# A complex-gated linear attention with a GEGLU layer behind it: group 5's q and k turned by TensorE in place of transposing DMAs, one PSUM copy per turned group, and a new written order

## The chip, the cores and the metric

One core of one Trainium2 chip. A core has five engines that run side by side, each through its own instructions in order, and wait for one another by semaphores: TensorE (PE; its weight loads are shown apart as PEld), VectorE (DVE), ScalarE (ACT), GpSimd (POOL) and SyncE (SP). SP computes nothing; its queue issues DMAs, as POOL's does too. The metric is the device time of one execution in microseconds: the median of several runs, and beside it one execution under the hardware profiler.

## The reference

```python
# q, k, v, a_re, a_im: 4 batches x 8 heads x 768 steps x 48
mag = sqrt(a_re**2 + a_im**2)
scale = minimum(mag, 0.999) / (mag + 1e-06)
ar, ai = a_re * scale, a_im * scale
for t in range(S):                       # one 48 x 48 state per batch and head
    new_re = ar[t] * S_re - ai[t] * S_im
    new_im = ar[t] * S_im + ai[t] * S_re
    S_re, S_im = new_re + outer(k[t], v[t]), new_im
    y[t] = q[t] @ S_re
x = y as (4 * 768) x (8 * 48)
ffn = (gelu(x @ w_gate) * (x @ w_val)) @ w_out      # 384 -> 1536 -> 384
out = x + sigmoid(x @ w_res) * ffn
```

The gates are a complex number of modulus under one for each step, head and row of the state. The kernel doesn't step through time. It takes log and angle of the gates, sums them along time by matmuls with triangular matrices, and multiplies q by the running product and k by its inverse, with cosine and sine; within a block of steps attention is then a masked product of q and k, and a state is carried from block to block.

## The kernel before

The 768 steps of four batches are cut into 12 groups of 256 steps: group p is batch p mod 4, stretch p div 4. A group has two chunks c of 128 steps. Eight units of the second layer follow: units 0 to 3 take one group each (0 to 3), units 4 to 7 two each (4 and 5, 6 and 7, 8 and 9, 10 and 11).

All work is cut into named steps (`Steps.add`), and a string `ORDER` (L288) names the steps in the order in which they are written out, for all engines at once. No scheduler moves anything: each engine runs its steps in the order of that string (L946), and waits where the data or a buffer isn't ready. A dictionary `eo` in `PARAMS` says for many steps which engine does them. The names have the group or unit first, then the chunk, then the half of the heads.

- Loads, issued by SP: `Lar`, `Lai`, `Lq`, `Lk`, `Lvf`, 192 KB each. `VC` casts v to bf16. Weights, issued by POOL: `Wg0` to `Wg3`, `Wv0` to `Wv3`, `Wr`, `Wo0` to `Wo2`. `HOLDW` and `HOLDO` (L909) are one-element copies on POOL that wait for a certain load, so that what POOL issues behind them starts later.
- Gates (L539): squares `SQR`, `SQI`; their sum `ADD` on DVE; logarithms and exponentials `LNR`, `EXR`, `LM` and the arctangent `ATN` on ACT; the ratio `TH` on DVE; sums along time `CSL` (log) and `CST` (angle) on PE; from CSL `EX` and `EI` on ACT (the tiles E and Ei); from CST `OFF` (ACT or DVE) and `FR` and `ABS` on DVE, then `SIN` and `COS` on ACT. `CR`, `CD` carry the angle, and `DR`, `DS`, `DE`, `DI`, `DT`, `ML`, `ME`, `MM`, `MN` the moduli, from one stretch to the next.
- `log`, `trig` and `gelu` in the order load ACT's table for what follows (L949).
- Products (L700): `QE`, `KE` multiply q and k by E and Ei, `QR`, `KR` by cosine and sine into the tiles padQ and padK, all on DVE.
- Turning q and k: groups 0 to 4 on PE. `TP` makes eight 128x96 transposes for four heads, q's into the first half of a PSUM bank and k's into the second (L745), and two `CP` copies of 96x512, each on an engine of its own, bring them to the tile qk. From group `turn` = 5 on, `QT` and `KT` (L718) are transposing DMAs, one for a whole group's q and one for its k, into QT and KT.
- Attention (L722): `AT` multiplies turned q and k (L759), `AM` masks on DVE (L762), `DK` forms the new part of the state, `MI`, `ED`, `EN`, `EB` bring the state forward, `Y` forms the output of a chunk and `X` copies it to x. x is turned by PE for groups 0 to 4 (`XT`, copy `XC`) and by a transposing DMA from SP from group 5 on (`XD`, L829).
- The second layer (L824): `GP` and `VP` multiply by w_gate and w_val (L848), `GE` is the GELU on ACT, `HM` the product on DVE (L859), `RP` and `SG` the residual gate, `OP` the product with w_out (L873), `OT` and `RX` the last two elementwise steps, `ST` the store.

Tiles come from rings: a pool has as many buffers as `bufs` says, and each new tile takes the next one. PSUM has four banks in one ring (`psM`, tag mm) for CSL, CST, GP, VP, RP, OP, TP and XT, two for AT and one each for Y and DK.

Of the kernel before, what the change touches and what calls it, by code (L numbers as in the profile page):

```python
# [10 lines left out]
FP = mybir.dt.float32  # L11
# [7 lines left out]
 'turn': 5,  # L19
# [34 lines left out]
 'cpe': ('ACT', 'DVE'),  # L54
# [10 lines left out]
 'eo': {'CP0.0.0.0': 'ACT',  # L65
        'CP0.0.0.1': 'DVE',
        'CP0.0.1.0': 'ACT',
        'CP0.0.1.1': 'DVE',
        'CP0.1.0.0': 'DVE',
        'CP0.1.0.1': 'DVE',  # L70
        'CP0.1.1.0': 'ACT',
        'CP0.1.1.1': 'DVE',
        'CP1.0.0.0': 'DVE',
        'CP1.0.0.1': 'DVE',
        'CP1.0.1.0': 'DVE',
        'CP1.0.1.1': 'ACT',
# [24 lines left out]
        'CP4.1.0.0': 'DVE',
        'CP4.1.0.1': 'ACT',
        'CP4.1.1.0': 'DVE',
        'CP4.1.1.1': 'DVE',
        'CRA10': 'DVE',
        'CRA11': 'DVE',
        'CRA4': 'POOL',
        'CRA5': 'POOL',
        'CRA6': 'POOL',
        'CRA7': 'POOL',  # L110
        'CRA8': 'DVE',
        'CRA9': 'POOL',
# [4 lines left out]
        'CRB4': 'POOL',  # L117
        'CRB5': 'POOL',
        'CRB6': 'DVE',
        'CRB7': 'DVE',  # L120
        'EB10': 'POOL',
# [3 lines left out]
        'EB6': 'DVE',  # L125
        'EB7': 'POOL',
        'EB8': 'POOL',
        'EB9': 'ACT',
# [3 lines left out]
        'EN5': 'DVE',  # L132
# [3 lines left out]
        'EN9': 'POOL',  # L136
        'MM10': 'DVE',
        'MM11': 'DVE',
# [3 lines left out]
        'MM7': 'DVE',  # L142
        'MM8': 'POOL',
        'MM9': 'DVE',
        'MN10': 'POOL',
        'MN11': 'POOL',
        'MN4': 'POOL',
        'MN5': 'POOL',
        'MN6': 'POOL',
        'MN7': 'DVE',  # L150
        'MN8': 'POOL',
        'MN9': 'POOL',
        'OFF0.0': 'DVE',
# [60 lines left out]
        'SQR0.0': 'DVE',  # L214
        'SQR0.1': 'ACT',
        'SQR1': 'DVE',
        'SQR10': 'ACT',
        'SQR11': 'DVE',
        'SQR2': 'DVE',
        'SQR3': 'DVE',  # L220
        'SQR4': 'ACT',
        'SQR5': 'DVE',
        'SQR6': 'ACT',
        'SQR7': 'DVE',
# [4 lines left out]
        'VC1.0': 'DVE',  # L229
# [3 lines left out]
        'VC11.0': 'POOL',  # L233
        'VC11.1': 'ACT',
        'VC2.0': 'POOL',
        'VC2.1': 'POOL',
# [4 lines left out]
        'VC5.0': 'POOL',  # L241
        'VC5.1': 'ACT',
        'VC6.0': 'POOL',
        'VC6.1': 'POOL',
        'VC7.0': 'DVE',
        'VC7.1': 'POOL',
        'VC8.0': 'POOL',
        'VC8.1': 'ACT',
        'VC9.0': 'ACT',
        'VC9.1': 'POOL',  # L250
        'X0.0': 'ACT',
        'X0.1': 'ACT',
        'X1.0': 'ACT',
# [5 lines left out]
        'X2.0': 'ACT',  # L259
# [4 lines left out]
        'X4.1': 'ACT',  # L264
        'X5.0': 'DVE',
        'X5.1': 'ACT',
# [8 lines left out]
        'XC0.0': 'ACT',  # L275
        'XC0.1': 'ACT',
# [4 lines left out]
        'XC3.0': 'DVE',  # L281
        'XC3.1': 'DVE',
        'XC4.0': 'DVE',
# [82 lines left out]
class Steps:  # L366
# [24 lines left out]
def kernel(  # L391
# [15 lines left out]
    DD = 2 * D  # L407
# [574 lines left out]
```

## Time and profile before

| | |
|---|---|
| median of 3 runs | 274.76 us (274.43 to 276.25) |
| profiled execution | 275.13 us, span 273.4 us |
| PE busy | 234.9 us (86%) |
| DVE busy | 222.7 us (81%) |
| ACT busy | 207.9 us (76%), of it 34 table loads 43.6 us |
| POOL busy | 114.7 us (42%) |
| mean granted TensorE clock | 0.963 of full speed |

In the table of slices the span is cut into 40 equal parts of 6.8 us; a digit is the busy share of an engine in tenths, 9 for 90% or more, and in the row PEclk the TensorE clock that was granted. In tables by stretch each engine has its busy time and, in brackets, its instructions. The chain that ended last is followed back from the last instruction, at each step to what released it; its lines have start, length and what ran. A row of the groups of instructions has the count, the busy time, the mean of one in ns and the idle time of the engine just before them, with what ended it.

### The profile page before, as it was taken

How to read it: one execution, taken by the hardware profiler on the slowest of the kernel's cores; microseconds unless marked ns; L12 is line 12 of the kernel's file. 1: busy time of each engine (PE TensorE's matmuls, PEld its weight loads, DVE VectorE, ACT ScalarE, POOL GpSimd, SP SyncE). 2: the span in 40 equal slices, each digit the busy share in tenths (PEclk: the TensorE clock that was granted, in tenths of full speed). 3: DMA queues.
4: the chain of work that ended last, by engine and by line, in shares of the span. 5: the costliest groups of instructions: out<-in, count | busy, mean ns of one | idle time of the engine just before them, and what ended most of it. 6: DMA issues, size and time to landing. Idle time of an engine off the chain costs nothing.

```text
span 273.4 us, 5330 instructions
## 1 busy us (share of the span) xinstructions
PE 234.9 (86%) x1913; PEld 148.2 (54%) x1926; DVE 222.7 (81%) x369; ACT 207.9 (76%) x343; POOL 114.7 (42%) x164
## 2 busy tenths in 40 slices
PE   0636777978999899997999999899899889999993
PEld 0313546765867777675744565545556445654451
DVE  1888899698999998995899999778998698634534
ACT  5999997999899899797799798979569763124410
POOL 4001197451437798299464385400751250021001
PEclk9985599999999999998999999999999999999999
DMA  7999999999999789899789938697769937132002
GB/s 149 207 207 191 206 199 186 186 183 173 184 220 181 138 181 196 143 174 167 123 166 190 190 70 158 152 215 138 153 74 185 205 80 158 30 95 80 2 29 86
DMA packets 170714, 41.35 MB, mean 151 GB/s; under 512 B 162624, under 2 KB 170688, under 8 KB 170688
## 3 DMA queue, kind: packets, MB, share of 16 engines
q1 hardware_dynamic: 163200, 37.04, 70.1%
q0 software_dynamic: 7488, 3.97, 11.0%
q8 instruction: 15, 0.25, 0.4%
q14 instruction: 11, 0.09, 0.1%
HBM read 31.33 MB, written 4.76 MB: 132 GB/s over the span
## 4 chain that ended last, share of the span: by engine, by line
PE 45%; DMA 18%; ACT 15%; DVE 10%; issue 6%; POOL 3%; SPq 0%; DVEq 0%; ACTq 0%; POOLq 0%
PE gv L848 22%; PE sums L873 8%; DMA wo<-in_moe_w_out_dram 5%; PE sums L643 4%; PE sums L609 4%; DMA wr<-in_moe_w_res_dram 3%; ACT L949 3%; ACT CS L521 3%; DMA KT<-padK 3%; PE sums L863 2%; ACT m L521 2%; DMA xT<-x 2%; PE at L759 2%; DMA QT<-padQ 2%; DVE kE L705 2%
## 5 line engine op out<-in xcount | busy, mean ns | idle before, releaser
L859 DVE SCALAR_TENSOR_TENSOR h<-h,gv 128x512 bf16<-128x512 bf16 x72 | 47.1, 679 | 15.7 <-PE gv L848 15.5
L521 ACT ACTIVATE h<-gv 128x512 bf16<-128x512 f32 x72 | 41.0, 603 | 22.6 <-PE gv L848 21.9
L848 PE MATMUL gv<-xT,wg 128*128 128x256 bf16 (+1 forms) x284 | 52.7, 325 | 4.6 <-DMA xT<-x 1.6
L848 PE MATMUL gv<-xT,wv 128*128 128x256 bf16 (+1 forms) x279 | 55.1, 326 | 1.0 <-DVE h L859 0.6
L873 PE MATMUL sums<-wo,h 128*128 128x384 bf16 x288 | 49.2, 326 | 2.1 <-DMA wo<-in_moe_w_out_dram 1.1
L949 ACT ACT_TABLE_LOAD x34 | 43.6, 1283 | 1.3 <-PEq L966 0.7
L848 PEld LDWEIGHTS <-wg 128*128 128x128 bf16 x288 | 27.4, 98 | 24.0 <-issue 3.8
L873 PEld LDWEIGHTS <-h 128*128 128x128 bf16 x288 | 27.4, 98 | 20.5 <-issue 2.1
L848 PEld LDWEIGHTS <-wv 128*128 128x128 bf16 x288 | 27.2, 99 | 19.0 <-issue 3.8
L762 DVE TENSOR_TENSOR atm<-at,mask 128x512 bf16<-128x512 f32 x48 | 31.8, 681 | 5.5 <-PE at L759 5.2
L885 POOL TENSOR_TENSOR ot<-ot,x 128x384 f32<-128x384 f32 x14 | 14.2, 1019 | 40.0 <-DVE ot L878 39.9
L521 ACT ACTIVATE ar<-ar 128x768 f32<-128x768 f32 (+1 forms) x28 | 23.1, 833 | 0.0
L878 DVE SCALAR_TENSOR_TENSOR ot<-sg,sums 128x384 f32<-128x384 f32 x24 | 12.9, 547 | 10.2 <-PE sums L873 6.3
L532 POOL CAST v<-vf 128x384 bf16<-128x384 f32 x17 | 11.7, 692 | 21.8 <-DMA vf<-in_v_dram 20.7
L609 PE MATMUL sums<-m,lt 128*128 128x384 f32 x24 | 12.3, 600 | 9.0 <-ACT Ei L521 8.5
L643 PE MATMUL sums<-ai,ut 128*128 128x384 f32 x40 | 18.4, 545 | 0.9 <-DMA ai<-G 0.6
L693 POOL DMA_DIRECT2D ai<-G x16 | 14.1, 880 | 8.4 <-ACT ai L521 5.7
L531 ACT CAST x<-y 128x384 bf16<-128x384 f32 x22 | 10.5, 477 | 7.5 <-issue 5.0
L521 ACT ACTIVATE sg<-sums 128x384 f32<-128x384 f32 x24 | 11.7, 499 | 5.1 <-PE sums L863 5.1
L863 PE MATMUL sums<-wr,xT 128*128 128x384 bf16 x72 | 14.6, 325 | 0.6 <-DMA wr<-in_moe_w_res_dram 0.3
L688 POOL TENSOR_SCALAR G<-m 32x384 f32<-32x384 f32 x10 | 14.0, 1397 | 2.8 <-issue 2.1
L521 ACT ACTIVATE m<-m 96x8 f32<-96x8 f32 (+2 forms) x29 | 12.9, 466 | 2.7 <-DMA d<-m 1.1
(94 smaller groups left out, 466.4 us busy)
## 6 DMA issues: line engine op xcount, KB each, us to landing
ar<-in_a_re_dram SPq DMA_DIRECT2D x24, 192.0 KB, 3.8
ai<-in_a_im_dram SPq DMA_DIRECT2D x24, 192.0 KB, 4.0
k<-in_k_dram SPq DMA_DIRECT2D x24, 192.0 KB, 4.3
vf<-in_v_dram SPq DMA_DIRECT2D x24, 192.0 KB, 3.8
q<-in_q_dram SPq DMA_DIRECT2D x24, 192.0 KB, 4.1
out_dram<-ot SPq DMA_DIRECT2D x24, 192.0 KB, 2.5
wg<-in_moe_w_gate_dram POOLq DMA_DIRECT2D x4, 288.0 KB, 7.8
wv<-in_moe_w_val_dram POOLq DMA_DIRECT2D x4, 288.0 KB, 9.2
```

Source lines behind the costliest of these rows:

```text
L521: return nc.scalar.activation(out=out, in_=in_, func=func, **kw)
L609: st.add("CSL%d.%d" % (p, c), "PE", lambda c=c: nc.tensor.matmul(out=st["csl", (p, c)], lhsT=lmat[c], rhs=part(("m2", p), (c,)), start=Tru ...
L643: return r + [nc.tensor.matmul(out=o, lhsT=tmat[c if s == 0 else 1], rhs=part(("ai", p), (c,)), start=not both, stop=True)]
L688: st.add("CR%s%d" % (nm, p), cre, lambda: eng.tensor_scalar(out=row[96:128], in0=part(("m2", p), (c,))[96:128], scalar1=-2.0 * math.pi, sc ...
L693: st.add("CD%s%d" % (nm, p), "POOL", lambda: nc.gpsimd.dma_start(out=part(("ai", pn), (cn,))[0:1], in_=row[127:128], accum_op=OP.add), r=[ ...
L762: st.add("AM" + sfx, "DVE", lambda: nc.vector.tensor_tensor(out=st["atm", i], in0=st["at", i], in1=mask4, op=OP.mult), r=[("at", i)], w=[( ...
L848: st.add("%sP%d.%d" % (nm.upper(), u, f), "PE", lambda f=f, fs=fs, nm=nm, w=w: [nc.tensor.matmul(out=st[nm + "p", (u, f)][:, j * 256:j * 2 ...
L859: st.add("HM%d.%d" % (u, f), "DVE", lambda f=f, h2=h2: nc.vector.scalar_tensor_tensor(out=h2(), in0=h2(), scalar=0.5, in1=gv(("vp", (u, f) ...
L863: st.add("RP%d.%d" % (u, jj), "PE", lambda jj=jj: [nc.tensor.matmul(out=st["rp", (u, jj)], lhsT=st["xT", u][:, i, jj * 128:(jj + 1) * 128] ...
L873: st.add("OP%d.%d.%d" % (u, jj, hh), "PE", lambda jj=jj, fs=fs: [nc.tensor.matmul(out=st["op", (u, jj)], lhsT=st["h2", u][:, f, jj * 128:( ...
L885: st.add("RX%d.%d" % (u, jj), rese, lambda jj=jj, pc=(p, c), eng=eng: eng.tensor_tensor(out=st["ot", (u, jj)], in0=st["ot", (u, jj)], in1= ...
L949: nc.scalar.preload_act_table_set(tables[nm])
```

## The change

- `turn` becomes 6: group 5 is turned like groups 0 to 4, by four steps TP5 of eight transposes each, and QT5 and KT5 go.
- The two copies of a turned group of heads become one, 96x1024, on one engine: 20 of these 24 on DVE, 4 on ACT (before 29 and 11 of half the width).
- `ORDER` is written anew for all engines, and `eo` with it. ACT has 38 table loads in it, was 34.
- Rings are replaced by named buffers: the digits behind a colon in the order say which buffer each new tile of the step takes (`TP0.0.1:10`: bank 1 of the four, buffer 0 of qk). The number of buffers of each kind stays.
- The carry's scaling (`CR`) could now be put on ACT; no step is.

The diff, cut: of `ORDER` its beginning and, of each version, the lines around group 5.

```diff
- 'turn': 5,
+ 'turn': 6,
...
- 'cpe': ('ACT', 'DVE'),
...
 ORDER = """
-Lar0.0 log LNR0.0 SQR0.0 Lai0.0 SQI0.0 ADD0.0 LM0.0 Lar0.1 LNR0.1 EXR0.1 Lai0.1 SQI0.1 TH0.1 SQR0.1 EXR0.0 Lai1.1
-CSL0.0 Lai1.0 SQI1 TH0.0 Lar1.0 trig ATN0.1 ADD0.1 Lar1.1 SQR1 ATN0.0 log LM0.1 CST0.0 ADD1 LM1 EX0.0 CST0.1 CSL0.1
-OFF0.0 FR0.0 OFF0.1 Lk0.0 Lvf0.0 Lq0.1 CSL1.1 EI0.0 LNR1 EX0.1 VC0.0 DE0 EXR1 EI0.1 KE0.0 FR0.1 ABS0.1 TH1 trig COS0.1
-SIN0.0 ATN1 SIN0.1 CST1.0 CSL1.0 CST1.1 ABS0.0 COS0.0 Lar3.1 Lai4.1 Lai3.0 Lar3.0 Lai3.1 SQR3 SQI3 ADD3 KR0.0 log
...
-MM5 CRA6 MN5 gelu GE3.3 Lk9.0 GE3.5 Lk7.1 Lai11.1 QT5 Lvf5.1 Lar11.0 MI4 GP3.1 DK4.1 GP3.2 GE3.1 GE3.4 GE3.2 RP3.0
...
-Y4.1 DR8 EN5 HM3.3 KT5 VP3.4 DK5.0 XT4.0 AT5.0.0 AT5.0.1 DI6 HM3.1 DR9 log ML7 LM8 LM9 DT7.1 X4.1 ML6 ME6 ME7 HM3.4
...
-HM3.0 Y5.1 OFF6.1 RX2.0 DT7.0 DT6.1 trig ATN8 MM7 OFF7.1 ATN9 X5.1 FR7.1 FR6.1 ABS7 SIN6 ST2.0 XD5.0 OP3.1.0 OP3.0.0
-Lq6.0 Lq7.0 XD5.1 ABS6 XC4.1 GP4.2 Lar10.1 GP4.9 Lq7.1 ED5 COS7 KE6 VC6.1 OT3.1 OT3.0 DT6.0 MM6 MN6 EN6 GP4.10 GP4.3
...
+Lar1.0:0 Lai0.1:0 Lar0.1:1 log LNR0.1:0 EXR0.1 SQR0.1 SQI0.1:0 TH0.1 trig ATN0.1 CST0.1:0 Lai1.0:1 Lar0.0 Lai0.0
+Lar1.1 ADD0.1 Lai4.1:2 log LM0.1 CSL0.1:10 LNR0.0 Lai1.1 SQR0.0 EXR0.0 SQR1 SQI0.0 TH0.0 Lq0.1:0 Lar3.0:2 Lar2.1:3
+Lar3.1 SQI1:1 ADD0.0 Lq0.0 Lai5.1:3 Lvf0.1:0 VC0.1:0 trig ATN0.0 log LM0.0 EI0.1 CSL0.0:2 EX0.1 EI0.0 OFF0.1 SQR3
+CST0.0:3 ADD1 FR0.1 ABS0.1 OFF0.0 LNR1 EXR1 LM1 TH1 CSL1.0:111 FR0.0 trig SIN0.0:0 Lk0.0:0 Lk0.1 KE0.1 ABS0.0 COS0.0
+SIN0.1 COS0.1 Lai3.1:4 Lai3.0 KE0.0 SQI3:2 KR0.0 KR0.1 ATN1 ADD3 Lvf0.0:1 Lar4.1:1 Lai2.1:5 CSL1.1:0 Lar4.0 CST1.1:3
+log EX0.0 Lai4.0 QE0.0 QR0.0 CRB0 DE0:0 HOLDW Lar5.1:0 SQI4:3 OFF1.1 HOLDO VC0.0 FR1.1 QE0.1 Lar5.0 Lai2.0 CST1.0:2
+OFF1.0 LM3 EX1.0 EI1.0 LNR3 SQR4 TP0.0.1:10 TP0.0.0:31 QR0.1 FR1.0 CP0.0.1 EXR3 CP0.0.0 ABS1 AT0.0.1:00 Lar2.0
...
+SIN1:1 COS1 TP0.1.1:21 ATN3 VC1.0:1 DK0.0 CP0.1.0 Y0.0:0 AT0.1.0:10 CSL3.1:300 SQR5 CP0.1.1 QE1 CST3.1:1 MI0:0 AM0.1.0
+QR1 X0.0 OFF3.1 XT0.0:20 AT0.1.1:01 FR3.1 ADD2 AM0.1.1 log EI1.1 XC0.0 EI3.1 Lai5.0 Lk1.1 CSL3.0:1 CST3.0:0 KE1 Wg2
+LNR2 EXR4 EI3.0 EX3.0 Wg3 Wr KR1 Y0.1:1 TP1.0.0:20 DK0.1 Wg1 Wg0 X0.1 CP1.0.0 Wv3 Wv2 CRB1 DR4:0 DE1:1 XT0.1:1 EX3.1
+XC0.1 TP1.0.1:31 EXR2 ED0 OFF3.0 AT1.0.0:10 AM1.0.0 FR3.0 DK1.0 GP0.5:2 GP0.3:1 LM2 gelu GE0.3 ABS3 GE0.5 CP1.0.1
...
+SQI8:1 X4.1 RP3.1:3 TP5.0.0:10 TP5.0.1:21 ED4 CP5.0.0 CP5.0.1 CST7.0:0 GP3.2:1 VP3.1:2 SQR8 AT5.0.1:10 SG3.1 VC5.0
...
+Lq9.0:3 XC4.0 ML7 AM5.1.1 AM5.1.0 Y5.1:2 XT4.1:2 CST7.1:0 EXR8 ME6 ME7 ST2.0 HM3.0 HM3.3 X5.1 OFF7.1 FR7.1 Lai11.0 TH8
+trig COS6:1 ATN9 SIN6 MN6 XD5.1 Lk9.1:2 ST1.1 XC4.1 ABS7 OP3.1.0:3 OP3.0.0:1 VC11.0:3 QE6 OT3.1:1 OT3.0:2 SIN7:0 ATN8
...
-    def run(self, name):
+    def run(self, name, slots=""):
+        slots = iter(slots)
         for k in self.info[name][2] + self.info[name][4]:
             if k[:2] not in self.T:
-                self.T[k[:2]] = self.tiles[k[0]]()
+                self.T[k[:2]] = self.tiles[k[0]](slots)
...
-                for n, eng in enumerate(PARAMS["cpe"]):
-                    eng = on("CP%s.%d" % (sfx, n), eng)
-                    st.add("CP%s.%d" % (sfx, n), eng, lambda n=n, eng=eng: copy(
-                        eng, st["qk", i][0:DD, n * 512:n * 512 + 512], st["tp", i][0:DD, n * 512:n * 512 + 512]),
-                        r=[("tp", i)], w=[("qk", i, n)])
+                cpe = on("CP" + sfx, "DVE")
+                st.add("CP" + sfx, cpe, lambda cpe=cpe: copy(cpe, st["qk", i][0:DD], st["tp", i][0:DD]),
+                       r=[("tp", i)], w=[("qk", i)])
```

More of the change, by code (lines that the diff above doesn't have):

```diff
@@ L116 @@
         'CRB3': 'POOL',
-        'CRB4': 'POOL',
+        'CRB4': 'DVE',
         'CRB5': 'POOL',
-        'CRB6': 'DVE',
-        'CRB7': 'DVE',
-        'EB10': 'POOL',
+        'CRB6': 'POOL',
+        'CRB7': 'POOL',
+        'EB10': 'ACT',
         'EB11': 'POOL',
@@ L124 @@
         'EB5': 'POOL',
-        'EB6': 'DVE',
-        'EB7': 'POOL',
+        'EB6': 'POOL',
+        'EB7': 'ACT',
         'EB8': 'POOL',
-        'EB9': 'ACT',
+        'EB9': 'POOL',
         'EN10': 'POOL',
@@ L131 @@
         'EN4': 'POOL',
-        'EN5': 'DVE',
+        'EN5': 'POOL',
         'EN6': 'POOL',
@@ L228 @@
         'VC0.1': 'POOL',
-        'VC1.0': 'DVE',
+        'VC1.0': 'POOL',
         'VC1.1': 'POOL',
@@ L232 @@
         'VC10.1': 'ACT',
[L233 to L236, printed above, removed]
+        'VC11.0': 'DVE',
+        'VC11.1': 'POOL',
+        'VC2.0': 'DVE',
+        'VC2.1': 'ACT',
         'VC3.0': 'POOL',
@@ L258 @@
         'X11.1': 'DVE',
-        'X2.0': 'ACT',
+        'X2.0': 'DVE',
         'X2.1': 'ACT',
```

355 lines of the change are left out of this document (172 added, 183 removed).

## The prediction

> **What bounds the kernel now.** I read the table of slices first, then busy time by stretch, then the chain that ended last.
>
> ```profile
> PE   0636777978999899997999999899899889999993
> DVE  1888899698999998995899999778998698634534
> ACT  5999997999899899797799798979569763124410
> PEclk9985599999999999998999999999999999999999
> ```
>
> PE is busy 86% of the span, and the first quarter is where it is not: there ACT and DVE are full while PE waits for them. From 66.7 us on PE has work nearly always. No engine has room in the middle:
>
> ```profile
> 75.00:125.00 50.00, 47.49 (x509) 35.96 (x507) 47.99 (x83) 46.12 (x78) 34.71 (x48) 1.00 0.95 175
> 125.00:135.00 10.00, 8.31 (x81) 5.81 (x82) 6.43 (x12) 6.91 (x15) 6.13 (x11) 0.83 1.07 162
> 140.00:175.00 35.00, 34.08 (x267) 19.49 (x270) 34.30 (x54) 31.92 (x55) 17.44 (x23) 1.00 0.81 155
> ```
>
> The columns are length, PE, PE weight loads, DVE, ACT, POOL, granted clock, DMA share and GB/s. Between 75 and 125 us PE is busy 95%, DVE 96%, ACT 92%; between 140 and 175 us 97%, 98% and 91%. Between 125 and 135 us all three drop, and the chain says why:
>
> ```profile
> 49.40 14.20 DMA wo<-in_moe_w_out_dram
> 63.64 1.47 PE sums L873 x8
> ...
> 119.20 7.44 DMA KT<-padK
> 126.69 0.62 PE at L759 x8
> ```
>
> The first pair: unit 0's output waits until the last piece of w_out lands at 63.6 us. The second: group 5's k is turned by a DMA issued at 119.20 and landed at 126.64, and PE stands for it. Looked at by the microsecond, the stretch is:
>
> ```profile
> 125.00:126.00 1.00, 0.00 (x0) 0.00 (x0) 0.79 (x2) 0.22 (x2) 0.95 (x2) 1.00 1.44 108
> 126.00:127.00 1.00, 0.31 (x6) 0.31 (x7) 0.00 (x0) 0.96 (x2) 1.00 (x3) 1.00 1.02 125
> 127.00:128.00 1.00, 1.00 (x8) 0.70 (x6) 0.65 (x2) 1.00 (x3) 1.00 (x2) 0.63 1.27 257
> 128.00:129.00 1.00, 1.00 (x2) 0.46 (x2) 1.00 (x3) 0.73 (x4) 1.00 (x2) 0.50 1.10 191
> 129.00:130.00 1.00, 1.00 (x4) 0.39 (x3) 0.10 (x1) 0.59 (x3) 1.00 (x3) 0.50 1.05 196
> ```
>
> After the idle 1.7 us the granted clock falls to 0.5 until about 130.3 us.
>
> From 139.5 us (first gate matmul of unit 4) to the end at 268.7 us PE is idle about 5 us in all; what starts there late ends late.
>
> **The change part by part.**
>
> *The wait for KT5 goes.* PE gets back 1.73 us of idle time, and the half clock of 127.3 to 130.3 us (1.0 − 0.63 and twice 0.50, and 0.34 of the next: about 1.7 us of work lost). I take −3.5 us. The low bound is −1.7 (another gap brings the clock down anyway). What is late next: X5.1, whose turned copy landed at 139.38 before, 0.1 us ahead of unit 4's first matmul. It hangs on AT5 and so moves forward too.
>
> *32 transposes on PE.* A row "PE tp L745 x8" of the chain is 0.45 us at full clock (89.32); four such steps are +1.8 us. At the early half clock they take about 0.95 each, so the bounds are 1.8 and 3.8. They stand in a stretch where PE is busy 95%.
>
> *One copy per turned group.* No 96x1024 copy is in the trace. On DVE 96x512 takes 412 ns and the 128x384 copy out of PSUM 348 ns, so 128 columns are 64 ns and 1024 columns about 670; bounds 412 (width is free) and 824 (two copies). On ACT 578 and 489 give about 930; bounds 578 and 1156. Before: 29 x 412 + 11 x 578 = 18.3 us on the two. After: 20 x 670 + 4 x 930 = 17.1 us, of which DVE +1.4, ACT −2.6. A group of q and k no longer waits for the later of two engines (3.6 us of idle DVE time were put down to ACT's half), but now waits 0.67 for one. Nearly nothing, and it is in the sums below.
>
> *New order, start.* SP's queue now loads group 1's half first, and ACT's first activation needs the third load. The loads land about 0.9 us apart (a median of 3.8 after issue), so ACT starts at about 5.7 in place of 3.57. Before q of group 0 is rotated (QR0.0) ACT loads a table seven times, was four. Walked in order, with 0.46 for an activation of 384 columns, 0.74 for 768, 1.28 for a table and 2.4 us from LM to the exponentials behind CSL (12.49 to 14.87 in the trace): LM0.0 ends at 15.9, the exponentials of the second half at 18.3, EX0.0 at 27.3, QR0.0 (DVE) at 28.4. The first transposes then stand behind EX1.0/EI1.0, which free their bank, so at about 29.3; before, 25.09. Going on in ACT's order the first GELU starts at 48.5 instead of 45.06, and DVE's copy for unit 0 comes about 4 us later. But the weights still land at about 63.6: POOL's queue puts the first weight behind HOLDW and VC1.0 (about 33 us, was 23.08), yet eleven of the twelve landed after 39 us before, one every 2 to 3 us, and the last is issued near 50 (49.40 before). Behind that gate ACT's work to unit 1's first GELU sums to 67.5 to 68.8 (before 67.66), and PE's to 67.5 (66.7). So of 4.2 us late I carry +1.0; bounds 0 and 4.2.
>
> *New order, middle.* Sums of the steps in written order, each step at its own duration or its group's mean, from unit 1's first gate step to unit 4's: PE 61.3 to 62.7 (the transposes less what moved), ACT 73.5 to 74.9, DVE 74.1 to 73.9 (counted to unit 3's first output). All three are over 90% busy: +1.0 of the 1.4; bounds 0 and 3.8 (transposes at half clock).
>
> *New order, rest.* From unit 4 on PE's sum is 120.0 to 120.4: +0.4. ACT has 38 tables to load, was 34; two of the four stand between unit 4's and unit 5's first GELU. They take 2 x 1.28 = 2.6 us there:
>
> ```profile
> L949 ACT ACT_TABLE_LOAD x34 | 43.6, 1283 | 1.3 <-PEq L966 0.7
> ```
>
> ACT's idle time between 141.7 and 178 us was 36.3 − 33.0 = 3.3 us, which covers them if it falls right. I take half, +1.3; bounds 0 and 2.6. The row also says that ACT stood 1.3 us in all before 34 loads. The Trainium skill ("ScalarE: Activation LUTs", section "What ACT_TABLE_LOAD costs") gives the same 1283 ns, and a drain of 1380 ns for every switch on top; by it the sum would be some 2.8 us higher, by the row it is not, and the trace does not show that drain.
>
> *Explicit buffers.* PE's waits for a free bank in the middle were 0.8 behind OT, 0.2 and 0.2 behind ACT: at most −1.2, at least a like loss; I take 0.
>
> Sum: −3.5 + 1.0 + 1.0 + 0.4 + 1.3 = **+0.2 us**. The profiled execution took 275.13 (span 273.4 and 1.7 around it); 275.3 against that. The median shown is 274.76, 0.4 lower, so 274.9.
>
> **The rivals.**
>
> 1. *The late start is carried whole.* One mechanism: unit 0's elementwise work, not w_out, ends last before its output. Then 4.2 stands for 1.0: 274.9 + 3.2 = **278.1**, slower. It decides if unit 0's last product (HM0.0; 61.0 us before) comes later than the landing of w_out by over 2 us. For it: DVE is about 4 us late there. Against: ACT and DVE stood 1.7 and 3.1 us between 45 and 65 us, and ACT's two blocks of GELU are now one.
> 2. *The change doesn't do what it says.* The wait moves from KT5 to the transposing DMA of X5.1, through which unit 4 still goes. It landed with 0.1 us to spare, so if X5.1 is not earlier the −3.5 does not come: **278.4**. For it: SP's queue has loads and a store ahead of that DMA. Against: the sums put AT5 earlier.
> 3. *Gain whole.* w_out covers all of the late start, and idle ACT and DVE time covers the additions: −3.5 + 0.4 = −3.1, **271.6**. For it: the idle time named above. Against: engines busy 91 to 98% rarely take in work for nothing.
> 4. *A table load holds ACT longer than its row.* If each of the four held it as long again, 4 x 1.28 = 5.1 with half on the path: +2.6, **277.5**. Against: the row above. The skill's drain would be this rival's reason.
>
> **How the numbers follow.** Forecast, no change: 0.44, with its own range 272.5 to 277.4. Rivals: 0.17, 0.13, 0.23, 0.03. One percent, about what a measurement of this kernel can tell from no change, is 2.75 us: 272.0 to 277.5. So faster 0.23, same 0.44, slower 0.33. The range takes in rivals 3 and 1, 2 with the bounds of the transposes and tables: 270.8 to 280.3.
>
> **What would show it.** The start: the first transposes near 29 us and the first GELU near 48.5. The gate: unit 0's output waiting for w_out near 63.6 (rival 1: for DVE, later). KT5: no idle PE of over 1 us nor a clock under 1.0 between 110 and 140 us; first gate matmul of unit 4 near 138.5 to 140 (rival 2: behind xT, over 141). Copies near 670 ns. Tables: PE idle in 140 to 180 us of 3 us or less. The forecast is wrong if a new wait, of any kind, stands in the middle, where nothing hides it, or if PE's idle time from unit 4 on is not near 5 us.

## The result and the profile after

The kernel before took 274.19 us (median of 20 runs, 272.95 to 277.22), the changed kernel 277.41 (20 runs, 274.54 to 279.87). The ratio is 1.0077, with a 95% interval of 1.0049 to 1.0105: by it 2.1 us longer, under the 1% that the prediction called no change, though the interval reaches a little over it. The ratio leaves out executions over 1.5% above the fastest of the same kernel, as slow: one of the kernel before and five of the changed one, among them the one that was profiled, at 279.04 us (span 277.3). A second comparison, told below, came to 1.0021 (0.9994 to 1.0048). So two questions stand: where the gain on group 5 went, and why the same kernel differs so much from one execution to the next.

The page of the changed kernel, table of slices (40 slices, 6.9 us each):

```profile
PE   0447779995999999999889899995999999999993
DVE  0658999894899999998999999899887899623834
ACT  3989999888689989999989899984879752225310
PEclk9999956997999999999999999999999999999999
```

PE's 7 in the 19th slice, where it had stood for group 5's k, is now a 9. In exchange it has a 5 in the tenth slice (62 to 69 us), with the clock at 7 there, and another 5 in the 28th (187 to 194 us). The same by stretch:

```profile
60.00:65.00 5.00, 3.18 (x35) 2.12 (x33) 4.33 (x9) 2.98 (x7) 0.00 (x0) 1.00 1.27 191
65.00:70.00 5.00, 3.98 (x19) 2.25 (x20) 1.40 (x2) 4.97 (x7) 3.05 (x4) 0.66 0.92 178
75.00:125.00 50.00, 48.81 (x537) 37.77 (x536) 49.20 (x80) 47.37 (x79) 29.90 (x41) 1.00 0.88 164
125.00:135.00 10.00, 10.00 (x113) 8.08 (x110) 9.19 (x16) 9.74 (x20) 6.18 (x8) 1.00 0.45 82
140.00:175.00 35.00, 33.10 (x261) 18.59 (x263) 34.62 (x53) 32.49 (x55) 21.39 (x30) 1.00 1.01 173
```

Between 125 and 135 us PE is busy 10.00 of 10 us (8.31 before) at full clock (0.83): the wait for k's transposing DMA is gone. In the middle DVE is at 98% and PE at 98%. What is new stands in the chain that ended last:

```profile
55.99 9.99 DMA wo<-in_moe_w_out_dram
66.02 3.60 PE sums L867 x12
...
180.85 3.93 DVE padK L709
...
188.20 4.26 DMA QT<-padQ
```

The last piece of w_out was issued at 55.99 and landed at 65.98 (49.40 and 63.60 before). PE waited 2.85 us for it, and its first twelve products then took 3.60 us where twelve take 2.11 at full clock. This landing, behind which unit 0's output stands, is called the gate of w_out below; it is another thing than a gate step, which is a step GP. And one rotation on DVE, group 8's k, took 3.9 us where the others take 0.96; k's and q's transposing DMAs of group 8 stand behind it. The rows of the new copies and of the table loads, by form:

```profile
L943 ACT ACT_TABLE_LOAD x38 | 48.8, 1283 | 1.4 <-PEq L960 0.7
L525 DVE COPY qk<-tp 96x1024 bf16<-96x1024 bf16 x20 | 13.4, 680 | 1.2 <-PE tp L741 1.2
L524 ACT COPY qk<-tp 96x1024 bf16<-96x1024 bf16 x4 | 4.0, 1003 | 0.0
```

### The profile page after: what moved, and what is told of

It reads as the page before. It is cut to its first block, busy times and chain, and to the rows that moved or that the text cites. A ratio compares the mean times of both kernels' runs of the same rounds, so it can differ in the third digit from the quotient of the medians.

```text
span 277.3 us, 5362 instructions
## 1 busy us (share of the span) xinstructions
PE 240.0 (87%) x1945; PEld 150.7 (54%) x1958; DVE 227.4 (82%) x363; ACT 211.2 (76%) x339; POOL 110.5 (40%) x162
## 4 chain that ended last, share of the span: by engine, by line
PE 44%; DMA 18%; DVE 15%; ACT 9%; issue 9%; POOL 2%; SPq 1%; DVEq 0%; POOLq 0%; ACTq 0%
PE gv L842 17%; PE sums L867 13%; DMA wv<-in_moe_w_val_dram 4%; DMA wo<-in_moe_w_out_dram 4%; PE sums L857 3%; DMA wg<-in_moe_w_gate_dram 3%; PE sums L636 3%; PE sums L602 3%; ACT L943 2%; DMA out_dram<-ot 2%; PE at L753 2%; DVE qE L701 2%; DVE padK L709 2%; DVE kE L701 2%; DMA QT<-padQ 2%
## 5 line engine op out<-in xcount | busy, mean ns | idle before, releaser
L842 PE MATMUL gv<-xT,wg 128*128 128x256 bf16 (+1 forms) x281 | 53.4, 324 | 3.4 <-DVE h L853 0.8
L867 PE MATMUL sums<-wo,h 128*128 128x384 bf16 x288 | 50.6, 332 | 2.8 <-DMA wo<-in_moe_w_out_dram 2.8
L943 ACT ACT_TABLE_LOAD x38 | 48.8, 1283 | 1.4 <-PEq L960 0.7
L867 PEld LDWEIGHTS <-h 128*128 128x128 bf16 x288 | 28.1, 99 | 21.9 <-DMA wo<-in_moe_w_out_dram 3.0
L636 PE MATMUL sums<-ai,ut 128*128 128x384 f32 x40 | 19.3, 572 | 10.3 <-ACT ai L514 10.3
L514 ACT ACTIVATE ar<-ar 128x768 f32<-128x768 f32 (+1 forms) x32 | 26.0, 826 | 0.4 <-ACT Ei L514 0.3
L684 POOL TENSOR_SCALAR G<-m 32x384 f32<-32x384 f32 x11 | 15.2, 1384 | 27.0 <-DVE m L643 13.2
L525 POOL CAST v<-vf 128x384 bf16<-128x384 f32 x14 | 10.2, 726 | 22.5 <-DMA vf<-in_v_dram 22.2
L514 ACT ACTIVATE Ei<-sums 128x384 f32<-128x384 f32 x24 | 11.5, 487 | 7.4 <-PE sums L602 7.3
L709 DVE TENSOR_TENSOR padK<-CS,kE 128x1536 bf16<-128x1536 bf16 (+1 forms) x13 | 14.9, 1145 | 1.9 <-ACT CS L514 1.6
L801 PE MATMUL y<-v,atm 128*128 128x48 bf16 x192 | 13.0, 186 | 3.7 <-DVE atm L756 3.6
```

What stands on the lines that cost most here:

```text
L514: return nc.scalar.activation(out=out, in_=in_, func=func, **kw)
L636: return r + [nc.tensor.matmul(out=o, lhsT=tmat[c if s == 0 else 1], rhs=part(("ai", p), (c,)), start=not both, stop=True)]
L684: return engine(cre).tensor_scalar(out=o, in0=i, scalar1=-2.0 * math.pi, scalar2=None, op0=OP.mult)
L709: return nc.vector.tensor_tensor(out=pad, in0=st["CS", p][:, cs[0] * H:(cs[-1] + 1) * H], in1=sb, op=OP.mult)
L842: st.add("%sP%d.%d" % (nm.upper(), u, f), "PE", lambda f=f, fs=fs, nm=nm, w=w: [nc.tensor.matmul(out=st[nm + "p", (u, f)][:, j * 256:j * 2 ...
L867: st.add("OP%d.%d.%d" % (u, jj, hh), "PE", lambda jj=jj, fs=fs: [nc.tensor.matmul(out=st["op", (u, jj)], lhsT=st["h2", u][:, f, jj * 128:( ...
```

## The experiments

Four sets of runs were made, each on another chip. A ratio is always to the kernel before on the same chip, and a trace is one execution. The table has what the traces show: GB/s moved from 5 to 30 us, the landing of the last w_out, PE's wait for it, the first gate step of units 1 and 4 (its first weight load), and the span; times are in us.

| trace | GB/s | w_out | wait | unit 1 | unit 4 | span | ratio (95%) |
|---|---|---|---|---|---|---|---|
| before, first | 204 | 63.60 | 1.1 | 66.72 | 139.49 | 273.4 | 1 |
| changed, first | 200 | 65.98 | 2.8 | 71.78 | 142.09 | 277.3 | 1.0077 (1.0049 to 1.0105) |
| e1 changed, again | 220 | 62.55 | 0.4 | 66.68 | 136.88 | 271.6 | 1.0021 (0.9994 to 1.0048) |
| e2 two weights first | 210 | 62.66 | 0 | 67.02 | 137.33 | 273.0 | 1.0050 (1.0016 to 1.0084) |
| e3 POOL quiet | 213 | 62.78 | 0.6 | 66.91 | 137.32 | 270.3 | 0.9979 (0.9950 to 1.0009) |
| e4 old order, both parts | 210 | 64.06 | 1.3 | 67.19 | 138.26 | 271.2 | 0.9985 (0.9952 to 1.0017) |
| e5 before, again | 198 | 63.49 | 1.4 | 68.31 | 139.31 | 274.2 | one execution |
| e6 old order, turn | 208 | 63.60 | 0.4 | 66.72 | 138.44 | 272.2 | 1.0019 (0.9985 to 1.0053) |
| e7 old order, copies | 205 | 64.87 | 1.1 | 68.00 | 139.71 | 273.2 | 1.0045 (1.0007 to 1.0083) |
| e8 earlier start | 207 | 64.27 | 2.8 | 69.82 | 140.77 | 275.6 | 1.0083 (1.0050 to 1.0117) |
| e9 loads later | 204 | 60.94 | 0 | 65.85 | 137.39 | 271.7 | 0.9999 (0.9970 to 1.0027) |
| e10 loads later, POOL quiet | 207 | 60.17 | 0 | 65.54 | 137.04 | 269.6 | 0.9927 (0.9893 to 0.9960) |
| e11 w_out delayed | 211 | 66.69 | 5.0 | 73.50 | 144.27 | 277.1 | 1.0176 (1.0129 to 1.0222) |
| e12 three edits | 207 | 59.51 | 0 | 67.49 | 138.66 | 270.2 | 0.9927 (0.9890 to 0.9964) |

e1 to e4 ran on one chip, e5 to e8 on a second, e9 and e10 on a third, e11 and e12 on a fourth.

### e1: the changed kernel again

No edit.

> The changed kernel once more, nothing edited, to see which of its new waits recur. If the stretch of group 8's k rotation in unit 5 (3.92 us where such a rotation takes 0.96) is set by the written order (it starts while three POOL instructions stand ready back to back), it comes again within 0.5 us of that, with the PE idle of about 3.4 us around 188 to 193. If it was an accident of one execution it is below 1.5 us here and the time falls by about 2 us. The gate of w_out (last piece landing at 66.0, PE idle 2.9 us before the first output products, half clock behind them) is expected again in either case. Time against the kernel before: +1.5 to +3.5 us.

The stretch came again (3.56 us), with PE waits of 1.7 and 1.1 us behind it: it belongs to the order. The late landing of w_out didn't. From the stretches and PE's timeline of this second trace:

```profile
5.00:30.00 25.00, 11.75 (x24) 4.76 (x25) 16.59 (x29) 23.13 (x36) 2.12 (x5) 0.96 1.18 220
62.59 2.12 PE L865 MATMUL sums<-wo,h 128*128 128x384 bf16 x12 [0.41 <-DMA wo<-in_moe_w_out_dram]
```

and of the first:

```profile
5.00:30.00 25.00, 13.37 (x25) 5.34 (x26) 16.34 (x30) 23.32 (x36) 2.20 (x5) 1.00 1.02 200
66.02 3.60 PE L867 MATMUL sums<-wo,h 128*128 128x384 bf16 x12 [2.85 <-DMA wo<-in_moe_w_out_dram]
```

The last number of a stretch is GB/s. The loads ran at 220 in place of 200, group 1's v landed at 30.89 in place of 33.06, and POOL, whose first weight stands behind the cast of that v, began its weights 3.5 us earlier. They landed 3.4 us earlier, the wait shrank from 2.85 to 0.41 and the clock stayed up. Unit 1 began 5.1 us earlier, unit 4 5.2 and the end came 5.6 us earlier. Nearly all of the difference between the two executions is there at 66 us, and nothing later gave it back.

### e11: w_out delayed

```diff
-... GE0.2 Wv1 Wv0 RP0.0:0 Wo2 CRB3 ...
+... GE0.2 Wv1 Wv0 RP0.0:0 Wx0 Wx1 Wo2 CRB3 ...   # 384 and 192 KB that nobody reads
```

> The changed kernel with two more transfers (384 and 192 KB, into buffers that unit 1 uses later, read by nobody) issued between w_val and w_out, so that w_out lands later and nothing else of the order moves. At 2 us per 288 KB the last w_out lands about 4 us later than in the changed kernel's fast trace, near 66 to 67, as it did in its slow trace (66.0). Theory 'a late w_out is carried to the end': PE waits 3 to 4 us for it with the clock falling to about half behind the wait, unit 1's first gate step comes near 71 to 73 (66.7, 71.8 in the slow trace), and the end comes 4 to 6 us later, the ratio to the kernel before about 1.015 to 1.025. Rival 'the middle takes it up, and something else made the slow trace slow': unit 4's first gate step within 1 us of 136.9 and the end within 1.5 us.

```profile
65.00:70.00 5.00, 3.26 (x11) 1.58 (x12) 1.43 (x2) 4.97 (x8) 2.54 (x4) 0.54 0.88 166
66.74 4.02 PE L866 MATMUL sums<-wo,h 128*128 128x384 bf16 x12 [4.98 <-DMA wo<-in_moe_w_out_dram]
71.19 2.64 PE L866 MATMUL sums<-wo,h 128*128 128x384 bf16 x12
```

These are a stretch and two rows of PE's timeline. w_out landed 4.1 us later than in e1, the clock fell to 0.54 in 65 to 70 us, and the 24 products took 4.02 and 2.64 us in place of 2.12 and 2.11. Unit 1 came 6.8 us later (4.1 for the landing, the rest for the clock and the idle steps), unit 4 7.4 later, the end 5.5 later. A late w_out is carried, almost whole. The two traces are from two chips; the ratios, each to the kernel before on its own chip, say the same (1.0176 against 1.0021).

### e2: two weights ahead of the cast that waits

```diff
-... TP0.1.1:21 ATN3 VC1.0:1 DK0.0 ...          ... KE1 Wg2 LNR2 EXR4 EI3.0 EX3.0 Wg3 Wr ...
+... TP0.1.1:21 ATN3 Wg2 Wg3 VC1.0:1 DK0.0 ...  ... KE1 LNR2 EXR4 EI3.0 EX3.0 Wr ...
```

> The changed kernel with two of POOL's weight issues (two pieces of w_gate) moved ahead of group 1's cast of v, which stands waiting for its load until 33.1; nothing else. The weight stream then begins near 26.5 instead of 34.9. Theory 'the gate of w_out moved': two pieces land earlier at the 2 us per piece at which they land, so the last w_out lands at 61 to 63.5 instead of 66.0, PE's wait of 2.85 us and the half clock behind it go, unit 1's first gate step comes 3 to 5 us earlier (71.8 to 67-69), and the end comes 1 to 3 us earlier if unit 1 to 4 are bound by PE. Rival 'the middle is bound by the elementwise engines, which had already made up for it': unit 1 starts earlier, but unit 4's first gate step (142.1) moves by less than 0.8 us and the end by less than 0.8. Second rival 'the loads of groups 1 to 5 pay': two pieces (576 KB) take some 3 us of a DMA that is full, the first GELU (49.0) comes 1 to 3 us later and the end no earlier.

The second rival. The two pieces were issued at 25.1 and 25.9 and landed at 30.2 and 33.1, group 1's loads paid (its v 3.9 us later, the first GELU 0.95 later), and the last w_out landed where it had, at 62.66. The span grew by 1.35 us. The transfers are the limit there, not the issue: to bring w_out forward something else must move back.

### e9: the loads of group 2 held back

```diff
-... GE0.0 Lvf2.0:0 ... (Lq2.0 Lq2.1 Lk2.0 around it) ... DS4.0:0 VC1.1 VP0.1:1 ...   Lvf2.1:1
+... GE0.0 ... DS4.0:0 VC1.1 Lvf2.0:1 Lq2.0:2 Lq2.1 Lk2.0:2 VP0.1:1 ...               Lvf2.1:0
```

> The changed kernel with only the loads of group 2 (q, k and the first half of v, 960 KB, which now land one per 5 us beside the weights from 38.8 to 63) held back: its first v half goes into the buffer that group 1's second cast of v frees near 52, and stands ahead of the others in SP's order. Theory 'the landing of the last w_out sets the end': it lands at 59 to 61 instead of 62.6 (66.0 and 64.3 in the slower ones), PE has its first output product within 0.5 us of the last multiply of unit 0 (61 to 62) with no wait for w_out, unit 1's first gate step comes at 65 to 66.2 instead of 66.7 (71.8, 69.8), and the end is 1 to 2 us below the changed kernel's fast traces, 3 to 5 below its slow ones, its median 0.5 to 1% lower in relation to the kernel before. Rival 'group 2 is late instead': unit 1's first gate step comes earlier, but group 2's rotations (65.6 to 69.8) wait for q and k, DVE idles there, and unit 2's first gate step is not earlier than 92. Second rival 'the middle takes it up': all earlier until unit 1, but unit 4's first gate step within 0.7 us of 136.9.

The gate moved as meant: w_out at 60.94 with loads at only 204 GB/s, no wait, unit 1 at 65.85. But unit 2's and unit 4's first steps are about those of e1 (92.03 against 92.05; 137.39 against 136.88): ACT's first GELU of unit 1 came at 68.64 here, 68.56 there. Under some 62.6 us the landing no longer binds, ACT does (second rival). What the edit takes away is the wait where w_out is late: POOL's first weight was issued at 35.12 here, as late as in the first trace (34.90), and w_out still landed 5.0 us earlier than there. The forecast 0.5 to 1% did not come; the ratio, 0.9999, is not distinguishable from that of e1.

### e8: an earlier start

```diff
-Lar1.0:0 Lai0.1:0 Lar0.1:1 log LNR0.1:0 ... trig ATN0.1 ... log LM0.1 ... LNR0.0 ... trig ATN0.0 log LM0.0
+Lar0.1:1 Lai0.1:0 Lar0.0 Lai0.0 Lar1.0:0 ... log LNR0.1:0 ... LNR0.0 ... trig ATN0.1 ATN0.0 ... log LM0.1 LM0.0
```

> The changed kernel with the start mended: group 0's decays are loaded ahead of group 1's, and its first half no longer goes through a log, trig, log round of its own (one pair of table loads of 1.28 us less, 36 instead of 38). Group 0's second logarithm is then done near 12 instead of 16.3, the first transposes come 2.5 to 4 us earlier (29.2 to 25-27), the first GELU likewise (49.2 to 45.5-47). Theory of the forecast 'the late start is hidden, since unit 0's output waits for w_out anyway': last w_out still 62 to 63, unit 1's first gate step within 0.7 us of 66.7, the end within 0.8 us of the changed kernel's. Rival 'the late start is carried': the end comes 1.5 to 3.5 us earlier.

```profile
64.31 3.54 PE L865 MATMUL sums<-wo,h 128*128 128x384 bf16 x12 [2.78 <-DMA wo<-in_moe_w_out_dram]
```

The first transposes came at 27.13 (29.18 in e1) and the first GELU at 47.10 (49.24): 2.1 us won, less than I had written. Unit 0's last multiply ended at 60.21, and PE then waited for w_out until 64.31: the start was swallowed by the gate, as the forecast's step says. The time, 1.0083, says nothing for the start, and nothing against it: on this chip the loads moved at 198 to 208 GB/s, and the changed kernel itself was not run there. Nor can the rate and the edit's own order of loads be told apart: group 1's v landed at 32.13 here (30.89 in e1).

### e5, e6, e7, e4: the parts of the change in the old order

e5 is the kernel before, for a trace on the chip of e6 and e7.

> The kernel before, for a trace of it taken on the same chip as the runs beside it. In the first pair of traces the loads of the first 35 us moved at 190 to 205 GB/s under the changed kernel and its last w_out landed at 66.0; in its second trace they moved at 215 to 224 GB/s and it landed at 62.6, with unit 1's first gate step at 66.7 instead of 71.8. Theory 'the load rate is the chip's': here the kernel before also moves 210 GB/s or more in its first 25 us, its last w_out lands below 63.6, and unit 4's first gate step comes before 139.5. Rival 'the order sets it': rate and landing are those of its first trace within 0.5 us.

Its execution took 275.98 us, near the top of the 29 timed on that chip (271.87 to 276.32). Its loads moved 198 GB/s, and w_out landed at 63.49 (63.60 in its first trace). PE waited 1.41 us for it, the clock was 0.50 from 64 to 67 us, and unit 1 began at 68.31 in place of 66.72: the old order can lose time at this gate too. Taken with e4, e6 and e7, the old order's w_out lands between 63.5 and 64.9 at 198 to 210 GB/s; the unchanged new order's at 65.98, 62.78 (e3, the same there) and 62.55 at 200, 213 and 220. In these traces the new order's landing moves with the load rate, the old one's hardly.

e6 turns group 5 on PE in the old order:

```diff
-'turn': 5,
+'turn': 6,
-... KE5 ... QT5 ... KT5 ... AT5.0.0 AT5.0.1 ... Y5.0 HM3.5 X5.0 AT5.1.0 AT5.1.1 ...
+... KE5 ... TP5.0.0 TP5.0.1 CP5.0.0.0 CP5.0.0.1 CP5.0.1.0 CP5.0.1.1 ... AT5.0.0 AT5.0.1 ...
+... Y5.0 TP5.1.0 TP5.1.1 HM3.5 X5.0 CP5.1.0.0 ... CP5.1.1.1 ... XT4.1 AT5.1.0 AT5.1.1 ...
```

> The kernel before with only group 5 turned by TensorE, its eight copies of 96x512 all on DVE (0.41 each); the copies of groups 0 to 4 stay as they are. Theory of the forecast: PE's 1.73 us wait for group 5's k and the half clock behind it go, and about 3.3 us of DVE copies come in: the time is 1.5 to 3.5 us below the kernel before, and no slice between 120 and 145 shows a clock below 1. Rival 'DVE pays': the PE's wait goes, but DVE's 3.3 us stand in its place, and the time is within 1 us. From the earlier run (turn and merged copies together 0.15% below the kernel before) the parts add: if the turn alone is 0.5% or more below, the merged copies cost the rest.

Stretches and PE's waits from 110 to 145 us, first of e5:

```profile
125.00:130.00 5.00, 3.54 (x37) 2.62 (x35) 3.39 (x8) 4.32 (x11) 4.65 (x7) 1.00 1.20 172
130.00:135.00 5.00, 5.00 (x73) 3.80 (x71) 5.00 (x11) 4.30 (x7) 1.20 (x3) 1.00 1.00 172
PE at L759 <- DMA KT<-padK: 1.5, 1, 1.5
PE gv L848 <- DMA xT<-x: 1.3, 1, 1.3
```

then of e6:

```profile
125.00:130.00 5.00, 4.95 (x63) 3.91 (x60) 5.00 (x11) 4.94 (x12) 4.95 (x8) 1.00 0.21 48
130.00:135.00 5.00, 3.60 (x47) 2.47 (x46) 3.58 (x9) 2.15 (x4) 2.59 (x7) 1.00 0.57 101
PE y L814 <- DVE atm L769: 1.4, 1, 1.4
```

PE is busy some 8.5 of these 10 us in both. The wait for the DMA (1.5) is gone, and 1.4 us of waiting for the masked product of group 5's second chunk has come, some 7 us later (0.9 us in both traces of the changed kernel). A DMA turns both chunks at once. On PE the second chunk's turning must wait until Y5.0 has let go of the two qk buffers, and then transposes, copies, attention product, mask and Y5.1 follow one another: from Y5.0 to Y5.1, first weight load to first weight load, it is 3.3 us in both traces of the kernel before, 5.7 in e6 and 6.8 in both traces of the changed kernel. Part of e6's 5.7 is where I put the steps; the changed kernel's is its own. The time: 1.0019, no gain. And in e5 PE waits the 1.5 us with the clock at 1.00 throughout: the half clock behind that wait in the first trace didn't come again there.

e7 merges the copies of groups 0 to 4 and leaves the DMAs; e4 has both parts.

```diff
-CP0.0.1.0 SQR4 ABS1 QE0.1 CP0.0.1.1      # 96x512 each, on ACT and DVE
+CP0.0.1 SQR4 ABS1 QE0.1                  # 96x1024, on DVE; likewise for all 20
```

> The kernel before with only the merged copies: one 96x1024 on DVE (0.68) where a pair of 96x512 stood on ACT and DVE (0.41 each on DVE, some 0.6 on ACT), groups 0 to 4, 20 copies; group 5 still turned by DMA. DVE gets 20 times 0.68 less its 30 halves at 0.41, about 1.3 us more, ACT loses its 10 halves, about 6 us. Forecast's term: +0 to +0.8 us in all. Theory 'the copies are free': within 1 us of the kernel before. Rival 'a single copy delays the first attention product of every group by 0.3 us': +1 to +2.5 us, PE idle before the attention products of groups 0 to 4.

> The kernel before in its own order, with the two named parts of the change and not its new order: group 5 turned by TensorE (four groups of transposes where the k transposing DMA stood and behind group 5's first output), one copy of 96x1024 on DVE for each pair of 96x512 copies, the two transposing DMAs of group 5 left out. If the named parts bring what the forecast took for them (PE wait of 1.73 us and 1.7 us of half clock near 127 go, -3.5; the copies and transposes +0.4 to +1.0), the time is 1.5 to 3.5 us below the kernel before. If that wait was cover for other work, or moves to group 5's x, the time is within 1 us. If DVE, over 90% busy in the middle, pays for every copy (20 copies at 0.68 for the DVE halves at 0.41, and four groups more: about 7 us of DVE), it is 2 to 4 us above.

The merged copies alone cost 0.45% (0.07 to 0.83), about 1.2 us. The trace of e7 has unit 0's first gate step at 44.67 (43.45 in e5), and it has the wait for group 5's k once more, longer than in either trace of the kernel before and with half clock behind it:

```profile
PE at L716 <- DMA KT<-padK: 3.2, 1, 3.2
128.00:129.00 1.00, 1.00 (x3) 0.40 (x3) 1.00 (x3) 0.84 (x5) 1.00 (x3) 0.50 1.33 207
```

k landed when it did in e5 (127.21 and 127.16), but PE came to it earlier. As e7's one span (273.2) is shorter than e5's (274.2), no trace shows where its 1.2 us went. Both parts together are at 0.9985 (0.9952 to 1.0017): no change, the forecast's −3.5 is not there. e6 and e7 don't add up to e4 (1.0064 against 0.9985). That e4 has the merged copies without the wait of e7 would account for it; the two ran on different chips, so this is not shown. By it the turning would be worth some 1.6 us beside merged copies, and nothing beside the old ones.

### e3, e10, e12: DVE beside POOL

```diff
-... GP5.7:0 RX4.3 RP5.1:1 EB8:0 RP5.0:2 ... FR11.0 RX4.0 AT8.0.0:00 ...     # all three on POOL
+... log EI11.0 ... EX10.0 EB8:0 ...  HM5.10 RX4.3 RX4.0 ...                  # EB8 on ACT, RX4 on DVE
```

> The changed kernel with the three POOL instructions that stand beside group 8's k rotation taken away from there: the cast of group 8's state goes to ACT (behind group 10's exponentials), the two residual additions to DVE, behind unit 5's third multiply. Theory 'DVE waits for POOL': the rotation takes 0.95 to 1.0 us instead of 3.92, k's transposing DMA is issued 2.5 to 3 us earlier (near 182), PE's two waits near 188 to 193 (2.06 and 1.32) shrink to under 1 together, and the end comes 1.5 to 3 us earlier. Rival 'the rotation waits for its own operands (the cosines of ACT)': it stays above 3 us wherever POOL is. Second rival 'unit 5 gives it back': the rotation is short, but the end moves by less than 0.8 us, since groups 8 and 9 then wait for something else (their transposing DMAs one behind the other, the elementwise work).

DVE's and POOL's timelines of the changed kernel, first trace:

```profile
180.85 3.92 DVE L709 TENSOR_TENSOR padK<-CS,kE 128x1536 bf16<-128x1536 bf16 x1
181.15 1.49 POOL L879 TENSOR_TENSOR ot<-ot,x 128x384 f32<-128x384 f32 x1
182.01 1.07 POOL L525 CAST Gb<-G 96x384 bf16<-96x384 f32 x1
182.47 1.47 POOL L879 TENSOR_TENSOR ot<-ot,x 128x384 f32<-128x384 f32 x1
```

and DVE's of e3:

```profile
176.33 0.95 DVE L707 TENSOR_TENSOR padK<-CS,kE 128x1536 bf16<-128x1536 bf16 x1
```

With POOL quiet the rotation takes 0.95. In the changed kernel it ends 0.83 us behind the last of three POOL instructions that run without a gap (184.77; POOL's last ends at 183.94): DVE got its turn when POOL had none left. ACT's cosines, the rival, had nothing to do with it. The span is 1.4 us under e1's, the ratio 0.9979 against 1.0021 on the same chip. PE's wait of 1.7 for DVE went, the one of 1.1 for q's transposing DMA stayed. The gain came again in e10.

e10 is e9 with this edit, e12 puts two more residual additions on DVE (`RX5.1`, `RX5.2`), away from group 11's q product.

> Both edits that were worth something or should be: group 2's loads held back, and POOL quiet beside group 8's k rotation. If each works on a wait of its own and lag is carried from unit 1 to the end (as between the two traces of the changed kernel: 5.1 us at unit 1's first gate step, 5.6 at the end), the gains add: 1 to 2 us from the loads, 1.2 to 1.4 from unit 5, the time 0.7 to 1.2% below the kernel before. If the second only fills what the first leaves open, the time is that of the better one alone, 0.2 to 0.5% below the kernel before.

> The last kernel but one (group 2's loads held back, POOL quiet beside group 8's k rotation) with one more edit of the second kind: the two residual additions that POOL runs beside group 11's q product (2.82 us where such a product takes 0.95) go to DVE, some 8 us later. Theory 'DVE waits for POOL': that product takes at most 1.3 us, unit 6's multiplies come 1 to 1.5 us earlier, and the end 0.5 to 1 us below that kernel's, the ratio to the kernel before 0.988 to 0.992. Rival 'there is no path through it': the product is short and the end is the same within 0.4 us, 0.991 to 0.995; or DVE's two additions (1.1 us) cost what the product gains.

e10 takes 0.9927 of the kernel before (0.9893 to 0.9960), 272.11 us against 274.06, and by the ratios 0.72% less than e9 on the same chip: the quiet POOL holds beside the other edit. By its ratio this version is below the kernel before, and below the changed kernel, whose two intervals lie above it. What the loads of e9 add to it is not shown, as e3 and e10 ran on different chips and their intervals overlap. In e12 the q product is short (0.95 for 2.82), and from unit 5's first gate step to the end its trace is 0.9 us shorter than e10's (95.6 to 96.6); its first GELU came 1.6 us later for no reason that I found, and the ratio is the same 0.9927. Whether the third edit is worth anything stays open.

## Why the prediction was right, and where its steps were wrong

The forecast was no change: +0.2 us, 274.9. Measured were +0.77% and, on another chip, +0.21%. The answer is right; the terms are not all. That they added up so closely is partly luck: the KT5 gain was taken too high, the rest of the middle seemingly too low, and the wait beside POOL was in no term.

- **The KT5 wait, −3.5.** Mis-sized. Beside the old copies it was worth about nothing (e6: 1.0019, 0.9985 to 1.0053); beside merged copies perhaps 1.6 us, by e4 and e7 on two chips; in the changed kernel itself it was not tried alone. The wait of 1.73 us did go, and no clock under 1 shows in 110 to 140 us. But 1.7 of the 3.5 was a half clock that the second trace of the kernel before doesn't have behind the same wait (1.5 us, clock 1.00), though e7 has it. And "what is late next: X5.1" looked past what stands ahead of X5.1, the second chunk's turning in series behind Y5.0. Rival 2 had the right kind of thing, a wait that moves, and the wrong place.
- **Copies, nearly nothing.** 680 and 1003 ns against 670 and 930. The sum was right as an engine's sum; in the old order alone they cost 1.2 us (e7), where is not shown.
- **The start, +1.0.** One count was off: ACT's tables up to QR0.0 are seven, but five before, not four (at 22.77 us in the trace before). The walk held: first transposes 29.01 (near 29), first GELU 49.01 (48.5). That w_out's landing hides it held too, in e8 and in e1 (unit 1 at 66.68, 66.72 before). What failed is the sentence that the weights still land at about 63.6, the last issued near 50: issued at 55.99 and landed at 65.98 in the profiled execution, 53.21 and 62.55 in e1. The gate itself had become a matter of the load rate, since POOL's first weight stands behind the cast of group 1's v. I had seen that position and counted on the later pieces to catch up. By e1 and e11 this accounts for the 5.6 us by which the first profiled execution is the longer. That it is also behind the ratio of 1.0077 is likely but not shown, for the executions of that ratio left no trace; and that slower loads caused the late landing is read from the traces, not tried.
- **The middle, +1.0.** From unit 1's first gate step to unit 4's it is 72.8 and 71.0 us in the two traces before, 70.3 and 70.2 after: −0.7 to −2.6 for KT5 and the middle together, where −2.5 was forecast. The sum held, at one end of what was measured. The split can't be read from these runs; if the turning was worth little, as in e6, the rest of the middle was a gain and no loss of 1.0. Unit 4's first gate step, forecast for 138.5 to 140, stood at 142.09 and 136.88.
- **The rest, +0.4 and +1.3 for table loads.** From unit 4 to the end: 133.9 and 134.9 before, 135.2 and 134.8 after; −0.1 to +1.3. PE's idle time there is 6.1 and 4.8 us, near the 5 of before. But the forecast's sign that it is wrong, a new wait where nothing hides it, stood in unit 5: the rotation beside POOL, worth 1.4 us in the trace of e3. Without it this part is 132.9 (e3), a gain, which leaves little for the table loads to have cost (+1.3 was forecast); they were not taken away by themselves. Their row is 38 loads of 1283 ns with 1.4 us of idle time before all of them: no drain beyond that, as the prediction's sum had it.
- **Rival 1, the start carried whole.** Not through unit 0's elementwise work, which ended at 61.85 in the profiled execution (61.70 before), but its price was that of the w_out gate: 5.1 us at unit 1, carried.

## What to carry to other kernels

A wait that is removed is worth what comes next, and next is the whole chain behind it: walk it to the point where the old and the new path meet again, buffers included. Where a late transfer can bring the clock down, price its lateness at the landing plus the slow products behind it, and ask which piece of it is needed first and what the landing depends on (here on the rate of loads that stand ahead of it in another queue). Look for vector instructions on SBUF operands written beside runs of POOL work: one moved group of three POOL steps was worth more here (0.4% in e3, 0.7% in e10) than the turning of group 5 (e6: nothing).

## What the runs showed of the hardware

- DVE waited for POOL. Where POOL ran three instructions without a gap, a DVE product of two SBUF operands took until 0.8 us behind the last of them: 3.92, 3.56 and 2.82 us in place of 0.95. It isn't always the whole run. In the trace of the kernel before, a product took 2.27 us and ended 0.8 us behind the third of four such instructions (it began at 218.74 us), and the next product then waited for the fourth. DVE copies out of PSUM beside POOL kept their 0.67 to 0.69 us. The Trainium skill ("SBUF — State Buffer", section "Who interferes with whom") says that a DVE instruction with two SBUF inputs and a POOL instruction that reads SBUF exclude one another, the second to start waiting out the first. The traces agree on the exclusion (0.95 us without POOL, 3.92 beside it); on the order they don't settle it, for the product of 3.92 us is recorded as starting 0.30 us ahead of the first of the three.
- The clock went with how busy PE was, not with the length of a wait alone. For w_out it fell behind waits of 2.8 to 5.0 us (0.66, 0.78, 0.54 in 65 to 70 us) and behind one of 1.41 in e5, but not behind 1.29 in e4; for group 5's k it fell behind 1.73 and 3.2 us, not behind 1.5. In all fourteen traces the granted clock changes only at steps of 3.41 us. Of the steps at full clock, all 24 with PE busy under 40% were followed by half clock, none of the 906 with PE busy over 53%, and 13 of the 25 between. The step with the wait for group 5's k and the one behind it, first in the first trace of the kernel before, then in e5:

```profile
123.85:127.26 3.41, 1.68 (x30) 1.44 (x26) 1.94 (x4) 2.59 (x4) 3.06 (x5) 1.00 1.25 165
127.26:130.67 3.41, 3.41 (x10) 1.77 (x10) 1.75 (x3) 2.73 (x9) 3.24 (x5) 0.50 1.14 204
125.22:128.63 3.41, 1.95 (x24) 1.44 (x22) 2.12 (x5) 2.76 (x6) 3.22 (x5) 1.00 1.29 167
128.63:132.04 3.41, 3.41 (x42) 2.62 (x41) 3.09 (x6) 3.35 (x9) 2.57 (x4) 1.00 1.00 178
```

- The loads from 5 to 30 us moved at 204 and 198 GB/s in the two traces of the kernel before and at 200 and 220 in those of the changed one. In the changed order the slower trace has w_out landing 3.4 us later and its end 5.6 us later.
- Of w_out's three pieces the changed order issues last the one that the first product needs (in the old order another one is last, and PE did four products before it waited). Turning their order round was not tried.
